# Linear attention and an MLP mixer on one core: the second batch's loads moved from SyncE's queue to GpSimd's, between the weight pieces

## The chip, the cores and the metric

The kernel runs on one core of one Trainium2 chip. The time is the device time of one execution in microseconds (us). A profiled execution gives a trace of every instruction and of every DMA packet; its times run from the first instruction. TensorE is called PE, VectorE DVE, ScalarE ACT, GpSimd POOL and SyncE SP.

## The reference

```python
# attention, for q, k, v of 8 batches x 8 heads x 576 positions x 64
phi = lambda x: np.where(x > 0, x, np.exp(x) - 1.0) + 1.0
q_p, k_p = phi(q), phi(k)
kv  = np.einsum('bhsd,bhse->bhde', k_p, v)
z   = np.sum(k_p, axis=2)
num = np.einsum('bhsd,bhde->bhse', q_p, kv)
den = np.einsum('bhsd,bhd->bhs', q_p, z)[..., None] + 1e-06
x = (num / den), heads joined to 8 x 576 x 512
# mixer: w_tok1 576x256, w_tok2 256x576, w_ch1 512x1536, w_ch2 1536x512
h = np.maximum(x.transpose(0, 2, 1) @ w_tok1, 0.0) @ w_tok2
u = x + h.transpose(0, 2, 1)
out = u + np.maximum(u @ w_ch1, 0.0) @ w_ch2
```

All inputs and the output are float32.

## The kernel before

**Staging.** The work goes batch by batch (n = 0 to 7), with the next batch's attention laid into the matmuls of this batch's channel mixer. Each batch reads q, k and v in two halves, c = 0 and 1, of 576 KB each (four heads to a half). A half of k or q goes through ACT's exponential (`phi_exp`, L248), DVE's max(x, 0) + 1 (`phi_add`, L252) and DVE's minimum of the two (`phi_end`, L258). A half of v is cast to bf16 into `vs` (`vcast`, L271), on DVE where `ON_DVE` names it (1v0) and else on ACT (1v1). PE then transposes the q halves (`qtr_mm`, L316), forms kv (L298, tokens 1K) and the numerators.

**Names in the order.** `ORDER` (L65) is a hand-kept list of some 1,100 tokens, run in sequence under a manual schedule; each engine and each issuing queue takes its own instructions in that order. `1Lk0` issues the load of batch 1, k, half 0. `1kx0`, `1ka0` and `1kb0` are its three phi steps, `1v1` is the cast of v half 1, `1Q..` are the transposes and `1K` is kv. `0ma5` and `0mb5` are the two halves of the first channel product for columns 640 to 767 (L682), `0r5` reads it back with relu. `0q0` to `0q11` are the second channel product of batch 0 (L743). `G01` and the like are DVE's sums of blocks of w_ch1 (L893), for a product scheme with seven multiplications. `Aw00`, `Aw11`, `Aw01` and `Aw10` copy w_tok2 into `w2p` in another order, the first two on POOL, the others on DVE (L661). `A38`, `A39`, `A43` and `A40` are the products that read `w2p` (L634). `A19` is a pair of warm-up matmuls on zeros (L1088), which stand in the buffer that v of batch 1 is loaded to.

**The loads.** Batch 0's k and q halves are issued by SP. POOL issues v of batch 0 (in bf16, two halves) and all weights, which it converts from float32 to bf16 on the way: w_tok1, a small half of its last row (`w1t`), w_tok2, w_ch1 in four pieces of 384 columns (`load_wc1`, L1115, all rows), the other half of `w1t` (L1134), and w_ch2 in four pieces of 384 rows (`load_wc2`, L1120). A w_ch1 or w_ch2 piece is 768 KB read and 384 KB written. Of a piece i of w_ch1, columns 384 i to 384 i + 383 come; block sums `G0.` need pieces 0 and 2. A piece of w_ch2 serves three of `0q0` to `0q11`.

Later batches' loads are issued by SP through `load` (L221). Two tables put waits in front of loads: `GATE` makes SP hold 1k0 until w_ch1 piece 0 has landed, and 2q0 until w_ch2 piece 1 has; `WGATE` makes POOL hold w_ch2 piece 1 until 1v1 has landed. Since a queue is in order, what stands behind a held load is held with it. Tokens `B0`, `B1` and `B2` issue w_ch2 pieces 1 to 3.

POOL's transfers use eight semaphores in turn, so that each of its DMA issues waits for the eighth one before it to land; POOL's other work stands behind such a wait.

Of the kernel before, what the change touches and what calls it, by code (L numbers as in the profile page):

```python
# [64 lines left out]
ORDER = """A2 A0 A1 A3 A4 A5 A6 A8 A9 A7 A10 A12 A13 A14 A11 A16 A17 A15 1Lk0 Aw11 A21 Aw00 A20 A19 1Lk1 1Lv1 A23 A18 A22 A25 A26  # L65
A29 1Lq0 A24 A28 A27 A32 A30 A31 A32l A33 A34 A35 A36 A37 Aw01 Aw10 A38 A39 A43 A40 0gt A41 A42 At3 G01 G02 At2 0ma5
0ma4 0ma1 G03 0mb1 0gv 0r1 G04 0ma7 0mb7 0r7 1kx0 0mb4 0r4 0mb5 0ma2 0mb2 0ma0 1ka0 1kb0 0mb0 0ma8 0mb8 G21 G22 G24
0r0 0r5 0ma11 G23 0ma3 G11 G12 G13 1ka1 0r8 1Lq1 1Lv0 B0 B1 B2 0mb3 0r3 0mb11 0r11 0ma6 0ma9 0mb9 0mb6 0r2 0r6 0q0
1kx1 1v1 0r9 1qx0 1kb1 0q1 2Lq0 1qa0 1qb0 1qx1 0ma10 0mb10 1Q01 1Q00 0r10 1qa1 0q2 1Qc00 1Qc01 ws02 1qb1 1Q11 1Q10 1v0
1K 1Kc0 1Qc10 2Lq1 0q3 1Qc11 1Kc1 1n20 2Lv0 1n01 0q4 0q5 1nc01 1n00 0q6 2qx0 2qx1 2v0 1nc20 2Lk0 1nc00 1n10 0q7 1n11  # L70
2Lk1 0q8 0q9 1nc10 1nc11 1n21 0q10 2qa0 1nc21 1f0 1fr0 1f1 1fr1 ws04 2kx1 2qb0 2qa1 ws14 0q11 wt2 1h01 1h00 2qb1 0z1
1hu00 1h11 2Lv1 3Lq0 1h10 0z0 1hu01 1hu11 1t0 1t1 1g2 1hu10 1t2 1tc1 1t3 1tc0 1ma3 1ma1 1tc2 1tc3 1mb1 2qT1 2qT0 2kx0
1ma8 1ma4 3qx0 1mb4 0z3 3Lq1 1r1 1r4 1gu2 0ut 1ma2 1mb2 1mb3 1ma5 1mb5 1mb8 2ka0 1r3 ws24 2v1 2kb0 1ma9 2ka1 2kb1 0uc
3qx1 2K 2Kc1 3Lk1 1r2 0z2 1ma7 1mb7 2Kc0 ws00 ws10 3qa0 1r7 1mb9 1r9 3qb0 1ma0 1mb0 1r8 ws12 2n 3Lv0 1r5 ws34 1ma11
1mb11 2nd 2o1 1r0 2n1 T01 1r11 2ne 1ma6 2n0 1mb6 1p10 3v0 2n2 1ma10 1mb10 2o0 2f0 3Lk0 1r6 1r10 1p20 1p21 0o1 1p11
3Lv1 1w10 ws22 2fr0 3qa1 wt0 4Lv0 3qb1 1w20 T02 3kx0 1w13 2f1 4Lq1 3ka0 T00 G14 ws32 ws20 1c0 Tr02 3kx1 1w30 3kb0 1w23
1p50 ws30 3qT1 1w40 3qT0 3ka1 3kb1 1p51 2fr1 2g1 Tr01 Tr00 0o0 1c2 4qx1 2g0 1p60 2gu0 2uT0 1p30 3v1 2gu1 2uT1 4qa1
1p61 1eZ 3K 1hZ 1c1 3Kc1 1p31 1eY 1p70 3Kc0 1p71 3n 1eW 4Lv1 4v0 3nd 3ne 3o0 U00 4Lk0 U01 1p41 U02 3o1 3n1 2x01 4Lk1
2x11 2y01 3n2 1p40 3n0 2x12 2s1 2s2 2x02 V0 1eX 4Lq0 2y11 2x16 2y12 5Lv0 2s3 2y02 2x15 4v1 4qb1 2x06 2y16 4kx0 2x21
2x05 2y21 1hW 4ka0 2x17 2y15 2y17 4kb0 3f0 4qa0 5Lk0 2s4 3f1 2x26 2y06 2x07 2y05 2y07 4qx0 5Lq0 4qb0 4qT0 3fr0 4ka1  # L80
2x25 3fr1 1hY 2y26 1o 2y25 2x14 2x13 2y13 3gt 2x27 2y27 2x22 2y22 2x23 2x03 2y03 2p10 2y14 4kx1 4kb1 2x04 2y04 2x24
4qT1 3g0 2y23 2w10 3g1 2y24 2w12 2p20 2w20 2w22 2p11 2w30 3gu1 2p50 2p51 2c0 2p60 3uT1 3gt1 2p61 3gu0 2p21 2c1 3gt0
3uT0 4K 2eZ 2p70 4Kc1 2c2 2w40 3ut 2p71 4Kc0 4n 2eW 5Lq1 2p30 4nd 2hW 5Lk1 4ne 2p31 5Lv1 4n0 2p41 2hZ 4o0 4n1 2p40
3x11 3s1 3x21 4o1 3y11 3s2 3x01 4n2 5kx0 3x16 3x12 2eY 3y21 T12 3s3 5v0 2eX 2hY 3x15 3y12 3x05 3y16 3x02 5ka0 2o 3y01
3x26 3y02 6Lk0 3x25 3x06 5kb0 3y25 W0 3x22 3y26 5ka1 3x23 3y06 3x17 3y22 3y15 3x27 3s4 3y05 3x07 3y17 5kx1 T11 3y27
3x03 3y07 Tr12 6Lk1 3x14 Tr11 3y03 3x24 5kb1 3x13 3y24 4f0 3y13 5qx0 5qa0 4f1 3y14 3y23 4fr0 5qb0 3x04 4fr1 T10 3w12
3y04 5qa1 4g0 Tr10 3w10 5v1 4g1 4gu0 5qx1 3p20 4gu1 4uT0 5K 6kx1 3p21 3w20 4uT1 5qb1 3p10 5Kc1 6kx0 3w22 3p11 5qT1 3eZ
3p50 3c0 6ka1 3p51 5Kc0 5qT0 3w40 U10 3c2 3w30 U11 6Lq0 6Lq1 6kb1 U12 4s1 6ka0 3p31 V1 3p30 7Lk0 4s2 6Lv1 3p61 3eY
6Lv0 3p60 6kb0 7Lk1 5n 3c1 5nd 3hY 3p71 5ne 3p70 5n0 3hZ 4x02 5o0 3eW 4x01 4x21 5n2 4y01 3hW 3p40 4y21 4y02 4x06 6qx0
5n1 4x05 4x26 4y06 6qa1 3p41 4y05 5o1 4x11 4s3 4x03 3eX 4y11 4x25 4y26 4s4 3o 4x07 4y03 6qx1 4x12 4y07 4x16 4x27 4y25  # L90
4y12 4x04 4y16 6qb1 5f0 4y04 6qa0 6v0 4x15 4y27 4x23 4w10 4y15 4x17 6qb0 5fr0 4x22 4y17 4x13 6qT0 4x24 4y23 4x14 4y24
4y13 6qT1 5f1 4y14 4y22 6v1 7ka1 4p20 4w12 4p21 5fr1 4w20 5g1 4w22 4p10 5gu1 4p11 5g0 4w40 5uT1 4c0 4eZ 5gt 6K 5gu0
4hZ 4p50 6Kc1 6Kc0 5gt1 5uT0 7kx1 4p51 5gt0 4p60 4c2 4w30 7Lv0 6n 7kx0 7Lq0 7kb1 4p61 7Lq1 6ne 7Lv1 4p30 6nd 4c1 6n2
4p31 4p71 6n0 4p70 4eY 5x11 6o1 5x02 6o0 5y11 5s1 5x12 4eW 5x01 5s2 5x15 5y01 4hW 6n1 4p40 7v0 5x16 5y12 4p41 5y16
7ka0 5x06 5y15 5s3 5x21 5y02 7F12 5x13 5y21 4eX 4hY 5x17 5y06 5x05 5y17 5x26 5y05 7kb0 4o 5x07 5y26 5x25 5y13 5x03
5y25 5s4 5x27 7qa0 7qx0 6f0 5y07 7v1 7qb0 5x14 6f1 7qa1 7qx1 5y27 5x04 6fr0 5y03 5x22 6fr1 5x23 7qb1 5y14 5x24 5y22
5y04 7qT1 7K 5y23 5p10 7Kc1 7Kc0 5w10 7qT0 5y24 6g0 5w30 6g1 5w12 5w20 5p20 6gu1 5p50 5p11 5w22 6uT1 6gu0 5p21 5c0
5p51 5eZ 6uT0 5p60 5c2 5w40 7n 5hZ 7nd 5p61 7ne 5p31 7n1 5c1 7F15 5p30 7o1 7o0 5p70 7n2 5p71 6s1 5eY 6x21 6x01 6s2 5hY
7n0 6x11 6y01 6x12 6y11 6x06 6y21 6s3 6x15 5eW 6y06 6x16 6x02 5hW 6y16 6x05 6y02 5p40 6y12 7F14 6x26 6s4 6y15 6x17
7F11 6x25 6y26 6x07 7F10 6y05 5p41 6y25 W1 6x13 5eX 6x03 6y07 6x23 7F13 6x27 6y03 6x22 5o 6x04 6y22 7f0 6y17 6y23 7f1  # L100
7fr0 6y27 6y04 6x14 6y13 7fr1 6x24 6y14 6w30 7g0 6y24 6w10 6p10 7gu0 7g1 6w12 7uT0 6p11 6w20 6p50 6w22 6c0 5ut 6p20
7gu1 6p51 7F2 7uT1 7gt 6p61 7gt0 6p60 6w40 7x12 6c1 7gt1 6p21 6c2 7F4 7ut 6p71 6eZ 7x11 6p70 7s1 6hZ 7x02 6eW 7x01
# [9 lines left out]
def kernel(  # L112
# [108 lines left out]
    def load(nm, n, c, gate=None):  # L221
        src_ = src[nm][n].rearrange("(j a) (p t) d -> (a p) j (t d)", a=2, t=T)
        js = slice(2 * c, 2 * c + 2)
        return after(nc.sync.dma_start(out=raw[nm, rb(n)][:, js], in_=src_[:, js]), gate)
# [887 lines left out]
    NB = 4  # L1112
    CB = DCH // NB

    def load_wc1(i):  # L1115
# [1 line left out]
        return nc.gpsimd.dma_start(
            out=wc1[:, :, cs], in_=moe_w_ch1[:, cs].rearrange("(k p) c -> p k c", p=128))
# [76 lines left out]
```

## Time and profile before

| What | us |
|---|---|
| median of 3 runs (lowest, highest) | 245.59 (244.32, 246.74) |
| the profiled execution: its own time | 243.56 |
| its span, first to last instruction | 241.8 |
| PE busy in the span | 233.3 (97%) |
| DVE, ACT, POOL busy | 213.3, 136.6, 77.1 |
| DMA: share of 16 engines of SP's queue, of POOL's | 51.2%, 24.7% |

The granted TensorE clock was 0.999 of full. Busy time is that of instructions; waits and DMA issues show in other views. In a line of the timeline the first number is the start, the second the length of a run of like instructions; the bracket gives the idle time in front of it and what ended that. A line of a DMA issue tells when it was issued, not when the data landed; the view of DMA issues has the median time to landing.

### The profile page before, as it was taken

The page shows a single profiled execution, that of the slowest core. Times are in us where ns is not written, and L with a number is a line of the kernel's source. Part 1 is how long each engine was busy: PE and PEld are TensorE (multiplying, and loading weights), DVE is VectorE, ACT ScalarE, POOL GpSimd, SP SyncE. Part 2 cuts the span into 40 slices and gives each one's busy share as a digit, 9 for nine tenths or more (in the row PEclk, how much of TensorE's full clock was granted, in tenths as well). Part 3 has the DMA queues.
Part 4 walks back from the last instruction along what each step waited for, and adds up shares of the span by engine and source line. Part 5 has one row for each costly group of instructions (what it writes and reads, how often), then busy time and mean ns, then how long its engine had stood idle before and what let it go on. Part 6 is the DMA issues. An engine that isn't in the chain of part 4 may idle for free.

```text
span 241.8 us, 6383 instructions
## 1 busy us (share of the span) xinstructions
PE 233.3 (97%) x2616; PEld 173.5 (72%) x2616; DVE 213.3 (88%) x389; ACT 136.6 (56%) x224; POOL 77.1 (32%) x86
## 2 busy tenths in 40 slices
PE   7899979999999999999999999999999999999992
PEld 3585435465687677789877887688778867888882
DVE  5987897989899899999999999999999599867662
ACT  4763781788687296237994397448923542346100
POOL 8750046173800620035100620207005820440640
PEclk9999999999999999999999999999999999999999
DMA  6999999997998999488948989494782186134026
GB/s 241 273 202 253 333 295 291 411 206 215 338 313 122 287 359 274 87 124 304 294 122 173 367 266 199 82 276 164 159 139 46 39 171 119 22 80 96 3 55 207
DMA packets 49805, 48.42 MB, mean 200 GB/s; under 512 B 30064, under 2 KB 35568, under 8 KB 49776
## 3 DMA queue, kind: packets, MB, share of 16 engines
q1 hardware_dynamic: 41664, 35.00, 51.2%
q0 software_dynamic: 7472, 12.22, 24.7%
q10 hardware_dynamic: 640, 0.79, 1.1%
q8 instruction: 20, 0.33, 0.5%
q14 instruction: 9, 0.07, 0.1%
HBM read 35.85 MB, written 9.44 MB: 187 GB/s over the span
## 4 chain that ended last, share of the span: by engine, by line
PE 83%; DMA 7%; DVE 4%; POOL 3%; issue 1%; ACT 0%; POOLq 0%; DVEq 0%; ACTq 0%
PE ps L966 27%; PE ps L924 23%; PE ps L444 6%; PE ps L743 5%; PE ps L455 4%; PE ps L682 4%; DMA wc<-in_moe_w_ch_dram 4%; DMA k_raw<-in_k_dram 3%; PE ps L707 2%; PE ps L729 2%; PE ps L298 2%; PE ps L1020 2%; PE ps L383 2%; DVE swc L893 1%; DVE y L252 1%; POOL qT L1107 1%
## 5 line engine op out<-in xcount | busy, mean ns | idle before, releaser
L966 PE MATMUL ps<-k_raw,v_raw 128*128 128x256 bf16 x252 | 31.7, 273 | 0.0
L939 ACT COPY v_raw<-ps 128x512 f32<-128x512 f32 x30 | 16.9, 595 | 23.0 <-PE ps L924 21.7
L966 PEld LDWEIGHTS <-cr 128*128 128x128 bf16 x252 | 24.4, 98 | 5.3 <-DVE cr L677 0.3
L966 PEld LDWEIGHTS <-v_raw 128*128 128x128 bf16 x252 | 24.1, 98 | 3.6 <-issue 0.4
L924 PEld LDWEIGHTS <-swc 128*128 128x128 bf16 x240 | 23.3, 98 | 3.5 <-issue 0.4
L1067 POOL TENSOR_TENSOR obuf<-obuf,q_raw 128x512 f32<-128x512 f32 x6 | 8.2, 1373 | 48.7 <-DVE obuf L1060 48.7
L677 DVE CUSTOM_DVE_ANT_0 cr<-ps,v_raw 128x512 bf16<-128x512 f32 x30 | 20.1, 685 | 4.1 <-ACT v_raw L939 2.1
L924 PEld LDWEIGHTS <-wc 128*128 128x128 bf16 x216 | 21.1, 98 | 3.6
L924 PE MATMUL ps<-crt,swc 128*128 128x256 bf16 x180 | 23.3, 273 | 0.0
L248 ACT ACTIVATE e<-q_raw 128x1152 bf16<-128x1152 f32 x16 | 18.7, 1167 | 6.8 <-DVE x L360 4.8
L682 PE MATMUL ps<-uT,wc 128*128 128x512 bf16 x96 | 22.1, 380 | 0.0
L966 PE MATMUL ps<-wc,cr 128*128 128x256 bf16 x168 | 21.6, 273 | 0.0
L248 ACT ACTIVATE e<-k_raw 128x1152 bf16<-128x1152 f32 x16 | 18.7, 1170 | 3.2 <-DMA k_raw<-in_k_dram 3.1
L924 PE MATMUL ps<-uT,wc 128*128 128x256 bf16 x144 | 19.5, 273 | 0.0
L1060 DVE TENSOR_TENSOR obuf<-ps,u 128x512 f32<-128x512 f32 x24 | 16.4, 685 | 2.9 <-PE ps L966 2.7
L409 DVE TENSOR_TENSOR x<-ps,dens 128x768 bf16<-128x768 f32 x18 | 16.5, 934 | 0.0
L1067 POOL TENSOR_TENSOR obuf<-obuf,part 128x512 f32<-128x512 f32 x6 | 7.7, 1287 | 27.1 <-DVE dens L396 18.6
L1067 POOL TENSOR_TENSOR obuf<-obuf,w 128x512 f32<-128x512 f32 x6 | 7.8, 1292 | 26.3 <-ACT w L1054 19.5
L682 PEld LDWEIGHTS <-wc 128*128 128x128 bf16 x96 | 9.0, 98 | 9.8
L466 DVE TENSOR_TENSOR u<-ps,x 128x1024 bf16<-128x1024 f32 x12 | 14.5, 1220 | 0.3 <-PE ps L455 0.2
L832 DVE TENSOR_TENSOR v_raw<-cr 128x512 bf16<-128x512 bf16 (+3 forms) x24 | 14.4, 619 | 0.0
L444 PE MATMUL ps<-x,w 128*128 128x512 bf16 x56 | 14.4, 379 | 0.0
(169 smaller groups left out, 510.2 us busy)
## 6 DMA issues: line engine op xcount, KB each, us to landing
k_raw<-in_k_dram SPq DMA_DIRECT2D x16, 576.0 KB, 6.5
q_raw<-in_q_dram SPq DMA_DIRECT2D x16, 576.0 KB, 6.0
v_raw<-in_v_dram SPq DMA_DIRECT2D x14, 576.0 KB, 7.2
out_dram<-obuf POOLq DMA_DIRECT2D x12, 512.0 KB, 5.8
wc<-in_moe_w_ch_dram POOLq DMA_DIRECT2D x8, 384.0 KB, 9.9
out_dram<-obuf POOLq DMA_DIRECT2D x4, 256.0 KB, 6.9
cr<-in_v_dram POOLq DMA_DIRECT2D x2, 288.0 KB, 7.5
out_dram<-obuf POOLq DMA_DIRECT2D x4, 128.0 KB, 4.8
```

What stands on the lines that cost most here:

```text
L248: nc.scalar.activation(out=ebuf[EBUF[f"{n}{nm}{c}"]], in_=f, func=AF.Exp)
L409: nc.vector.tensor_tensor(out=xv[:, :, rc0:rc0 + 3], in0=nd_tile(n, m)[:, :, k0:k0 + 6, 0:D].rearrange("p i (q a) d -> p i q a d", a=2), i ...
L444: nc.tensor.matmul(out=banks(f"{n}f")[:, mt], lhsT=w1t[:, b, ms] if r == R else w1[:, r, ms], rhs=x[b][:, r, :], start=(r == 0), stop=(r = ...
L466: nc.vector.tensor_tensor(out=u[b][:, rs], in0=banks(f"{n}g{i}"), in1=x[b][:, rs], op=ALU.add)
L677: nc.vector._custom_dve(TENSOR_ADD_SAT, out=o, in0=ps, in1=c, s0=3.4028234663852886e38, s1=0.0)
L682: nc.tensor.matmul(out=bank(f"{n}m{mc}"), lhsT=wc1[:, kj, 128 * mc:128 * mc + 128], rhs=uTj[b][:, kj] if n < 2 - U1 else uT[b][:, :, kj], ...
L832: return engine.tensor_tensor(out=s_[which - 1][:, ks], in0=x_, in1=y_, op=op)
L924: nc.tensor.matmul(out=ps[:, j], lhsT=lhs[:, k_, 128 * j:128 * (j + 1)], rhs=rhs[:, :, k_], start=(first and j == 0 and k_ == 0), stop=(k_ ...
L939: nc.scalar.copy(out={1: c1, 6: c6, 5: c5}[i], in_=ps)
L966: nc.tensor.matmul(out=ps, lhsT=lhs[:, k_], rhs=rhs[:, k_], start=(first and not skip and k_ == 0), stop=(k_ == KH - 1), skip_group_check= ...
L1060: nc.vector.tensor_tensor(out=slots(f"{n}P", 4)[:, d::2, HC[c]], in0=pair_tile(n, "X" if z == "W" else z), in1=u[n % 2][:, d::2, HC[c]], o ...
L1067: nc.gpsimd.tensor_tensor(out=o, in0=o, in1=part[i], op=ALU.add)
```

## The change

The six loads of batch 1 go out from POOL's queue, in a given place among the weight pieces, and the two gates that held 1k0 and w_ch2 piece 1 go.

```diff
-GATE = {'1k0': ('wc1', 0), '2q0': ('wc2', 1), '4q0': ('u', 2, 1), '7q0': ('u', 5, 1)}
-WGATE = {1: ('in', 'v', 1, 1)}
+GATE = {'2q0': ('wc2', 1), '4q0': ('u', 2, 1), '7q0': ('u', 5, 1)}
+WGATE = {}

-ORDER = """... A16 A17 A15 1Lk0 Aw11 A21 Aw00 A20 A19 1Lk1 1Lv1 A23 A18 A22 A25 A26
-A29 1Lq0 A24 A28 ...
-0ma4 0ma1 G03 0mb1 0gv 0r1 G04 0ma7 0mb7 0r7 1kx0 ...
-... 1ka1 0r8 1Lq1 1Lv0 B0 B1 B2 0mb3 0r3 ...
+ORDER = """... A16 A17 A15 A19 1Lk0 P2 1Lk1 P3 Pt 1Lq0 Aw00 Aw11 Pw 1Lq1 1Lv1 1Lv0
+B0 B1 B2 A21 A20 A23 A18 A22 A25 A26 A29 A24 A28 ...
+0ma4 0ma1 G03 0mb1 0gv 0r1 G04 0ma7 0mb7 0r7 1kx0 ...
+... 1ka1 0r8 0mb3 0r3 ...

     def load(nm, n, c, gate=None):
...
-        return after(nc.sync.dma_start(out=raw[nm, rb(n)][:, js], in_=src_[:, js]), gate)
+        queue = nc.gpsimd if n == 1 else nc.sync
+        return after(queue.dma_start(out=raw[nm, rb(n)][:, js], in_=src_[:, js]), gate)
...
-    for i in range(NB):
-        live["wc1", i] = load_wc1(i)
-    nc.gpsimd.dma_start(out=w1t[half[1], 1, :], in_=w1r[:, 2 * R])
-    load_wc2(0)
+    for i in range(2):
+        load_wc1(i)
+    for i in range(2, NB):
+        put(f"P{i}", load_wc1, i)
+    put("Pt", lambda: nc.gpsimd.dma_start(out=w1t[half[1], 1, :], in_=w1r[:, 2 * R]))
+    put("Pw", load_wc2, 0)
```

So POOL issues, after w_ch1 pieces 0 and 1: 1k0, w_ch1 2, 1k1, w_ch1 3, the rest of `w1t`, 1q0, the copies `Aw00` and `Aw11`, w_ch2 0, 1q1, 1v1, 1v0, w_ch2 1, 2 and 3. The warm-up pair `A19` moves ahead of `A20`, the first batch's kv of its first half (`kv_first(0)`, L565). The rest of the order is kept: DVE and ACT run the same instructions in the same sequence, ACT's being 1kx1, 1v1, 1qx0, 1qx1. SP's queue holds, after batch 0's four loads, the loads of batch 2 onwards.

More of the change, by code (lines that the diff above doesn't have):

```diff
@@ L63 @@
 4k1:0 5k0:0 5k1:0 5q0:0 5q1:0 6k1:0 6k0:0 6q1:0 6q0:0 7k1:0 7k0:0 7q0:0 7q1:0 25465:241833""".split())}
[L65 to L98, printed above, removed]
@@ L99 @@
-7n0 6x11 6y01 6x12 6y11 6x06 6y21 6s3 6x15 5eW 6y06 6x16 6x02 5hW 6y16 6x05 6y02 5p40 6y12 7F14 6x26 6s4 6y15 6x17
+ORDER = """A2 A0 A1 A3 A4 A5 A6 A8 A9 A7 A10 A12 A13 A14 A11 A16 A17 A15 A19 1Lk0 P2 1Lk1 P3 Pt 1Lq0 Aw00 Aw11 Pw 1Lq1 1Lv1 1Lv0
+B0 B1 B2 A21 A20 A23 A18 A22 A25 A26 A29 A24 A28 A27 A32 A30 A31 A32l A33 A34 A35 A36 A37 Aw01 Aw10 A38 A39 A43 A40
+0gt A41 A42 At3 G01 G02 At2 0ma5 0ma4 0ma1 G03 0mb1 0gv 0r1 G04 0ma7 0mb7 0r7 1kx0 0mb4 0r4 0mb5 0ma2 0mb2 0ma0 1ka0
+1kb0 0mb0 0ma8 0mb8 G21 G22 G24 0r0 0r5 0ma11 G23 0ma3 G11 G12 G13 1ka1 0r8 0mb3 0r3 0mb11 0r11 0ma6 0ma9 0mb9 0mb6
@@ new lines @@
+0r2 0r6 0q0 1kx1 1v1 0r9 1qx0 1kb1 0q1 2Lq0 1qa0 1qb0 1qx1 0ma10 0mb10 1Q01 1Q00 0r10 1qa1 0q2 1Qc00 1Qc01 ws02 1qb1
+1Q11 1Q10 1v0 1K 1Kc0 1Qc10 2Lq1 0q3 1Qc11 1Kc1 1n20 2Lv0 1n01 0q4 0q5 1nc01 1n00 0q6 2qx0 2qx1 2v0 1nc20 2Lk0 1nc00
+1n10 0q7 1n11 2Lk1 0q8 0q9 1nc10 1nc11 1n21 0q10 2qa0 1nc21 1f0 1fr0 1f1 1fr1 ws04 2kx1 2qb0 2qa1 ws14 0q11 wt2 1h01
+1h00 2qb1 0z1 1hu00 1h11 2Lv1 3Lq0 1h10 0z0 1hu01 1hu11 1t0 1t1 1g2 1hu10 1t2 1tc1 1t3 1tc0 1ma3 1ma1 1tc2 1tc3 1mb1
+2qT1 2qT0 2kx0 1ma8 1ma4 3qx0 1mb4 0z3 3Lq1 1r1 1r4 1gu2 0ut 1ma2 1mb2 1mb3 1ma5 1mb5 1mb8 2ka0 1r3 ws24 2v1 2kb0 1ma9
@@ new lines @@
+2ka1 2kb1 0uc 3qx1 2K 2Kc1 3Lk1 1r2 0z2 1ma7 1mb7 2Kc0 ws00 ws10 3qa0 1r7 1mb9 1r9 3qb0 1ma0 1mb0 1r8 ws12 2n 3Lv0 1r5
+ws34 1ma11 1mb11 2nd 2o1 1r0 2n1 T01 1r11 2ne 1ma6 2n0 1mb6 1p10 3v0 2n2 1ma10 1mb10 2o0 2f0 3Lk0 1r6 1r10 1p20 1p21
+0o1 1p11 3Lv1 1w10 ws22 2fr0 3qa1 wt0 4Lv0 3qb1 1w20 T02 3kx0 1w13 2f1 4Lq1 3ka0 T00 G14 ws32 ws20 1c0 Tr02 3kx1 1w30
+3kb0 1w23 1p50 ws30 3qT1 1w40 3qT0 3ka1 3kb1 1p51 2fr1 2g1 Tr01 Tr00 0o0 1c2 4qx1 2g0 1p60 2gu0 2uT0 1p30 3v1 2gu1
+2uT1 4qa1 1p61 1eZ 3K 1hZ 1c1 3Kc1 1p31 1eY 1p70 3Kc0 1p71 3n 1eW 4Lv1 4v0 3nd 3ne 3o0 U00 4Lk0 U01 1p41 U02 3o1 3n1
@@ new lines @@
+2x01 4Lk1 2x11 2y01 3n2 1p40 3n0 2x12 2s1 2s2 2x02 V0 1eX 4Lq0 2y11 2x16 2y12 5Lv0 2s3 2y02 2x15 4v1 4qb1 2x06 2y16
+4kx0 2x21 2x05 2y21 1hW 4ka0 2x17 2y15 2y17 4kb0 3f0 4qa0 5Lk0 2s4 3f1 2x26 2y06 2x07 2y05 2y07 4qx0 5Lq0 4qb0 4qT0
+3fr0 4ka1 2x25 3fr1 1hY 2y26 1o 2y25 2x14 2x13 2y13 3gt 2x27 2y27 2x22 2y22 2x23 2x03 2y03 2p10 2y14 4kx1 4kb1 2x04
+2y04 2x24 4qT1 3g0 2y23 2w10 3g1 2y24 2w12 2p20 2w20 2w22 2p11 2w30 3gu1 2p50 2p51 2c0 2p60 3uT1 3gt1 2p61 3gu0 2p21
+2c1 3gt0 3uT0 4K 2eZ 2p70 4Kc1 2c2 2w40 3ut 2p71 4Kc0 4n 2eW 5Lq1 2p30 4nd 2hW 5Lk1 4ne 2p31 5Lv1 4n0 2p41 2hZ 4o0 4n1
@@ new lines @@
+2p40 3x11 3s1 3x21 4o1 3y11 3s2 3x01 4n2 5kx0 3x16 3x12 2eY 3y21 T12 3s3 5v0 2eX 2hY 3x15 3y12 3x05 3y16 3x02 5ka0 2o
+3y01 3x26 3y02 6Lk0 3x25 3x06 5kb0 3y25 W0 3x22 3y26 5ka1 3x23 3y06 3x17 3y22 3y15 3x27 3s4 3y05 3x07 3y17 5kx1 T11
+3y27 3x03 3y07 Tr12 6Lk1 3x14 Tr11 3y03 3x24 5kb1 3x13 3y24 4f0 3y13 5qx0 5qa0 4f1 3y14 3y23 4fr0 5qb0 3x04 4fr1 T10
+3w12 3y04 5qa1 4g0 Tr10 3w10 5v1 4g1 4gu0 5qx1 3p20 4gu1 4uT0 5K 6kx1 3p21 3w20 4uT1 5qb1 3p10 5Kc1 6kx0 3w22 3p11
+5qT1 3eZ 3p50 3c0 6ka1 3p51 5Kc0 5qT0 3w40 U10 3c2 3w30 U11 6Lq0 6Lq1 6kb1 U12 4s1 6ka0 3p31 V1 3p30 7Lk0 4s2 6Lv1
@@ new lines @@
+3p61 3eY 6Lv0 3p60 6kb0 7Lk1 5n 3c1 5nd 3hY 3p71 5ne 3p70 5n0 3hZ 4x02 5o0 3eW 4x01 4x21 5n2 4y01 3hW 3p40 4y21 4y02
+4x06 6qx0 5n1 4x05 4x26 4y06 6qa1 3p41 4y05 5o1 4x11 4s3 4x03 3eX 4y11 4x25 4y26 4s4 3o 4x07 4y03 6qx1 4x12 4y07 4x16
+4x27 4y25 4y12 4x04 4y16 6qb1 5f0 4y04 6qa0 6v0 4x15 4y27 4x23 4w10 4y15 4x17 6qb0 5fr0 4x22 4y17 4x13 6qT0 4x24 4y23
+4x14 4y24 4y13 6qT1 5f1 4y14 4y22 6v1 7ka1 4p20 4w12 4p21 5fr1 4w20 5g1 4w22 4p10 5gu1 4p11 5g0 4w40 5uT1 4c0 4eZ 5gt
+6K 5gu0 4hZ 4p50 6Kc1 6Kc0 5gt1 5uT0 7kx1 4p51 5gt0 4p60 4c2 4w30 7Lv0 6n 7kx0 7Lq0 7kb1 4p61 7Lq1 6ne 7Lv1 4p30 6nd
@@ new lines @@
+4c1 6n2 4p31 4p71 6n0 4p70 4eY 5x11 6o1 5x02 6o0 5y11 5s1 5x12 4eW 5x01 5s2 5x15 5y01 4hW 6n1 4p40 7v0 5x16 5y12 4p41
+5y16 7ka0 5x06 5y15 5s3 5x21 5y02 7F12 5x13 5y21 4eX 4hY 5x17 5y06 5x05 5y17 5x26 5y05 7kb0 4o 5x07 5y26 5x25 5y13
+5x03 5y25 5s4 5x27 7qa0 7qx0 6f0 5y07 7v1 7qb0 5x14 6f1 7qa1 7qx1 5y27 5x04 6fr0 5y03 5x22 6fr1 5x23 7qb1 5y14 5x24
+5y22 5y04 7qT1 7K 5y23 5p10 7Kc1 7Kc0 5w10 7qT0 5y24 6g0 5w30 6g1 5w12 5w20 5p20 6gu1 5p50 5p11 5w22 6uT1 6gu0 5p21
+5c0 5p51 5eZ 6uT0 5p60 5c2 5w40 7n 5hZ 7nd 5p61 7ne 5p31 7n1 5c1 7F15 5p30 7o1 7o0 5p70 7n2 5p71 6s1 5eY 6x21 6x01 6s2
@@ L100 @@
+5hY 7n0 6x11 6y01 6x12 6y11 6x06 6y21 6s3 6x15 5eW 6y06 6x16 6x02 5hW 6y16 6x05 6y02 5p40 6y12 7F14 6x26 6s4 6y15 6x17
 7F11 6x25 6y26 6x07 7F10 6y05 5p41 6y25 W1 6x13 5eX 6x03 6y07 6x23 7F13 6x27 6y03 6x22 5o 6x04 6y22 7f0 6y17 6y23 7f1
```

## The prediction

> **What bounds the kernel now.** I read the busy time by stage first, to see where TensorE (PE) idles at all; columns are the stretch, its length, then busy us of PE, its weight loads, VectorE (DVE), ScalarE (ACT) and GpSimd (POOL), granted clock, DMA share, GB/s.
>
> ```profile
> 26.00:30.00 4.00, 4.00 (x20) 1.82 (x19) 3.90 (x10) 3.19 (x7) 0.00 (x0) 1.00 1.09 349
> 30.00:32.00 2.00, 1.29 (x7) 0.48 (x5) 2.00 (x4) 1.84 (x3) 1.03 (x2) 1.00 1.04 400
> 32.00:34.00 2.00, 1.69 (x8) 0.59 (x6) 1.86 (x3) 1.70 (x2) 1.46 (x2) 1.00 0.96 304
> 34.00:36.00 2.00, 1.74 (x17) 1.02 (x18) 1.86 (x4) 2.00 (x4) 0.00 (x0) 1.00 1.22 203
> 36.00:60.00 24.00, 24.00 (x294) 13.67 (x292) 21.15 (x43) 15.57 (x24) 10.76 (x11) 1.00 1.00 278
> 60.00:230.00 170.00, 170.00 (x1971) 135.20 (x1970) 157.39 (x276) 96.75 (x158) 47.59 (x49) 1.00 0.70 180
> ```
>
> From 36 to 230 us PE is never idle, so no later slack can win back a delay made before 36 us, and only the 0.71 + 0.31 + 0.26 = 1.28 us of idle in 30 to 36 us can be won there. The DMA engines are full (share about 1) to that point: it is a question of which bytes come first. Next, the timeline of PE (start, length, what; in brackets the wait before it and what ended it):
>
> ```profile
> 20.57 9.66 PE L682 MATMUL ps<-uT,wc 128*128 128x512 bf16 x44
> 30.94 1.89 PE L743 MATMUL ps<-wc,cr 128*128 128x512 bf16 x8 [0.71 <-DMA wc<-in_moe_w_ch_dram]
> 32.66 1.03 PE L682 MATMUL ps<-uT,wc 128*128 128x512 bf16 x4
> 34.14 0.68 PE L316 MATMUL ps<-identity,qp 128*128 128x128 bf16 x9 [0.45 <-DVE qp L258]
> ...
> 36.47 0.71 PE L298 MATMUL ps<-vs,kp 64*64 64x65 bf16 x64
> ```
>
> and of ACT, which feeds the transposes at 34.14, with the loads' issues on SP and POOL that feed ACT and PE:
>
> ```profile
> 29.52 1.17 ACT L248 ACTIVATE e<-k_raw 128x1152 bf16<-128x1152 f32 x1
> 30.57 1.15 ACT L271 CAST vs<-v_raw 128x1152 bf16<-128x1152 f32 x1
> 31.88 1.17 ACT L248 ACTIVATE e<-q_raw 128x1152 bf16<-128x1152 f32 x1 [0.16 <-DMA q_raw<-in_q_dram]
> 33.35 1.16 ACT L248 ACTIVATE e<-q_raw 128x1152 bf16<-128x1152 f32 x1 [0.30 <-DMA q_raw<-in_q_dram]
> ```
>
> ```profile
> 17.80 0.88 SPq L224 DMA_DIRECT2D k_raw<-in_k_dram  x2
> 18.73 0.47 SPq L224 DMA_DIRECT2D v_raw<-in_v_dram  x1
> 19.24 0.98 SPq L224 DMA_DIRECT2D q_raw<-in_q_dram  x2
> ```
>
> ```profile
> 11.07 0.74 POOL L1117 DMA_DIRECT2D wc<-in_moe_w_ch_dram  x1 [0.99 <-DMA cr<-in_v_dram]
> ...
> 15.26 1.54 POOL L661 COPY w2p<-w 128x320 bf16<-128x320 bf16 x2 [0.43 <-DMA w<-in_moe_w_tok_dram]
> ```
>
> See that ACT takes the value half 1v1 (30.57) before both query halves (31.88, 33.35), and that SP now issues 1v1 before 1q0 and 1q1.
>
> **Landings before and after.** Adding each issue's time to landing (DMA view by window): wc1 pieces 0 to 3 land at 17.8, 19.5, 21.5 and 26.0; 1k0 24.5, 1k1 28.4, 1v1 30.4, wc2 piece 0 30.9, 1q0 31.8, 1q1 33.3, 1v0 34.7, wc2 piece 1 36.8 (SP's gated issue of 2q0). Prices follow. A wc1 piece with its queue alone takes 1.9 us (17.8, 19.5, 21.5). A 576 KB load on SP's queue takes 1.45 us (batch two: issued 36.8 to 38.8, landing 42.8, 44.3, 45.6, 47.0, 48.4). A wc2 piece takes 2.05 (36.8, 38.9, 40.9).
>
> After the change SP's queue is empty from the first four loads until wc2 piece 1 lands, and one queue carries all: wc1 1 at 19.6, 1k0 21.1, wc1 2 23.0, 1k1 24.4, wc1 3 26.3, the small w1t half 26.5, 1q0 28.0, wc2 0 30.0, 1q1 31.5, **1v1 33.0**, 1v0 34.4, wc2 1 36.5. The total is the same bytes in the same time; the order differs.
>
> **Part by part.**
>
> *Gates removed.* SP's wait for wc1 0 and POOL's 14.2 us wait for 1v1 go. The chain's 6.74 us for 1k0 (17.80 to 24.54) goes: 1k0 is 3.4 us earlier. Late next is wc1 2.
>
> *Six issues move from SP to POOL.* POOL issues cost 0.54 to 0.86 us each, SP's 0.37 to 0.5. Each POOL issue also waits for the eighth POOL transfer before it (eight semaphores): 1k0 for v0 (about 11.1), 1q0 for w2 (15.2), 1v1 for 1k0 (21.1). Queued behind them on POOL are two w2p copies, once at 15.26, now after 1q0's issue: 15.6 + 0.75, so from 16.35, ends 17.1 and 17.9 (Aw00 now first). The second block of L634 products then starts 0.6 us late. Cover: PE waits for wc1 2 next. About seven transfers, 10 us, are ahead of each issue, so POOL's issue time itself costs nothing; were it stalled, that backlog must run out first.
>
> *One warm-up matmul pair moves ahead of kv_first(0).* At most 0.46 us (two steps of 0.23 from L1088, four in 1.11 us) on the first batch's chain; same cover. A gain is excluded, since it only goes ahead of work.
>
> *1k0 ahead of wc1 2.* 21.5 becomes 23.0. PE's fifth group of L682, 0ma7, is due at 20.57 + 4 x 0.44 = 22.3, so it starts 1.0 late (23.3); this covers the two delays above. DVE's first swc sum (21.48, which waited for the same piece) starts at 23.1, but 1k0's exponential was at 24.62 and moves 0.3 only. The 44 matmuls end near 31.2, wc2 0 is there at 30.0, and the 0.71 us wait is gone: PE's L743 starts at 31.2 against 30.94, +0.3. L682's last group ends near 33.9.
>
> *1q0 and 1q1 ahead of 1v1.* ACT, 1.0 late through PE, ends 1k1's exponential near 31.6 and then sits until 33.0, with 1q0 long landed behind it. The cast starts at 33.1 (+2.5). The first query exponential came 1.31 later, 0.16 of it waiting for data: now 33.1 + 1.15 = 34.25, **+2.35**. DVE's end of it and PE's transposes follow: 34.14 becomes 36.5, PE idle 2.6 us. The second half keeps the same spacing (compute-bound by DVE: 33.33 to 34.98 for its two ends), 1v0 is there at 34.4, so L298 at 36.47 becomes 38.8. wc2 1 is due after that and landed at 36.5. After it PE has work without pause, so 2.35 us stays.
>
> **Sum.** 1.0 for wc1 2, less 0.71 for wc2 0, is inside the 2.35, not added. The profiled execution's own time is 243.56 (span 241.8 and 1.8 around it): 243.56 + 2.35 = 245.9. It lay 2.03 below the median of 245.59; on the median, 247.9. I forecast that, 0.96% slower.
>
> The unknown is a plain f32 load's rate on POOL's queue, which before never makes one. Nearest rows: v0's two halves on that queue, 576 KB read each, land 1.65 us apart (10.85, 12.5) while sharing the engines; on SP's queue loads land 1.45 apart, at best 1.33 (4.54, 5.87). Five loads go up to 1v1's landing, itself included: 1.33 gives 0.6 less, +1.75; 1.65 gives 1.0 more, +3.35. Far row: out_dram stores of 512 KB on POOL's queue land 5.8 us after issue, two of them together, so at most 2.9 each: 7.25 more, +9.6. I take 1.45, the row of the same shape and bytes with its queue alone.
>
> **Rivals.**
> 1. *1v1 in time*: it lands by 31.6, so ACT never sits, and only wc1 2 costs, +1.0 through ACT: 244.6, on the median 246.6. For: 1.33 a load brings it to 32.4. Against: even that is 0.8 too late.
> 2. *Loads on POOL's queue are slower*, or POOL's issues stall past the backlog: v0's 1.65 a load gives +3.35: 246.9, median 248.95; far end 253.2 and 255.2. For: two POOL issues of 1.15 and 1.01 against 0.74. Against: the others hold 0.74 with DVE 88% busy (4.41 of 5 us in 10 to 15). [...]
> 3. *The clock falls in the new 2.6 us idle.* Price from rows: the PE work from the transposes to the end of L298, 34.14 to 37.2, at half speed costs up to 3.1 more: +4 to +5.45, I take +4.7: 248.3, median 250.3. Decides from: an idle long enough; the longest here after the start, 0.71, kept 1.00. [...]
> 4. *Not slower*: the queue without mixing runs faster. If 1v1 lands by 30.5, 2.5 earlier, and the pieces with it, the waits from 30.94 on go, at most 1.28 us: 242.3, median 244.3. It needs 12.7 us where I have 15.2 from wc1 0 on, a 20% better rate; share and GB/s (400 at 30 to 32 us) speak against.
>
> **Numbers.** About 1% is what a measurement of this kernel can tell from no change: bounds 243.1 and 248.05 on the median. Forecast 0.58, split about its mid 247.9 by some 0.6 for the landing and 1 for the runs: 0.32 within, 0.26 slower. Rival 1 0.11, within. Rival 2 0.14 and 3 0.07, slower. Rival 4 0.10: 0.06 within, 0.04 faster. So faster 0.04, within 0.49, slower 0.47. The range 245.6 to 250.4 reaches rival 1 less 1.0 for the runs and rival 3; it leaves out rival 4 and rival 2's far end.
>
> **What would show it.** Right: L682's 44 matmuls broken by a wait for wc near 22.5; no 0.71 wait at L743; ACT's cast of v_raw waiting some 1.4 us for in_v_dram until 33; PE idle over 2 us before L316; L298 at 38.8; nothing idle after. Wrong: v_raw landing before 31.6, loads spaced over 1.7 us, a clock under 1.00, or a gap after 40 us.

## The result, and the profile after

The changed kernel takes 247.04 us (median of 17 runs, 246.43 to 249.06); the kernel before, timed beside it, 245.28 us (17 runs, 244.03 to 247.53). The ratio is 1.0077, 95% interval 1.0049 to 1.0105: slower by 1.2 to 2.6 us. The forecast was 247.9, slower by 2.35.

The profiled execution after took 247.04 us with a span of 245.2. That of before took 243.56, less than any of its 17 runs here; so of the 3.48 us between the two profiles some 1.7 (245.28 - 243.56) belongs to that one quick execution of before, not to the change; where the other runs of before lose it, no trace shows. Of the 3.4 us between the two spans, 2.8 lie ahead of kv (L299) and 0.6 behind the last weight load, where before's profiled execution ends sooner than after's. Times on the traces are compared for their places, and the medians for the size.

Line numbers after are one higher than before from L224 on, as far as they are named here: L743 is now L744, L298 is L299.

The timeline of PE after (start, length, what, count; in brackets the wait before it and what ended it):

```profile
23.30 7.94 PE L683 MATMUL ps<-uT,wc 128*128 128x512 bf16 x36 [0.58 <-DMA wc<-in_moe_w_ch_dram]
31.08 1.89 PE L744 MATMUL ps<-wc,cr 128*128 128x512 bf16 x8
...
35.99 0.68 PE L317 MATMUL ps<-identity,qp 128*128 128x128 bf16 x9 [2.16 <-DVE qp L259]
...
39.27 0.78 PE L299 MATMUL ps<-vs,kp 64*64 64x65 bf16 x72 [0.95 <-DVE vs L272]
```

The 0.71 us wait of L743 for w_ch2 piece 0 is gone: L744 has no bracket. A wait of 2.16 us before the transposes (L317) and one of 0.95 before kv (L299) stand in its place. L299 starts at 39.27; before, its line stood at 36.47. Every weight load from L299 to the end comes 2.8 us later than the same one before.

Where the first wait comes from, in the timeline of ACT after:

```profile
32.92 1.16 ACT L272 CAST vs<-v_raw 128x1152 bf16<-128x1152 f32 x1 [1.23 <-DMA v_raw<-in_v_dram]
33.98 2.21 ACT L249 ACTIVATE e<-q_raw 128x1152 bf16<-128x1152 f32 x2
```

ACT stands 1.23 us for 1v1, and the two query exponentials run back to back behind the cast, with no wait for data of their own. Where the second wait comes from, in the timelines of DVE and of POOL after:

```profile
35.96 0.76 DVE L253 TENSOR_SCALAR y<-q_raw 128x1152 bf16<-128x1152 f32 x1
...
37.50 1.72 DVE L272 CAST vs<-v_raw 128x1152 bf16<-128x1152 f32 x1
```

```profile
36.86 3.36 POOL L813 TENSOR_TENSOR q_raw<-wc 128x512 f32<-128x512 bf16 x2 [8.45 <-DVE y L253]
```

The cast of 1v0 takes 1.72 us, where the same instruction took 0.76 before, and the two POOL sums of weights at L813 take 3.36 where they took 2.26. The same two in the timelines of DVE and of POOL before:

```profile
35.66 0.76 DVE L271 CAST vs<-v_raw 128x1152 bf16<-128x1152 f32 x1
```

```profile
36.90 2.26 POOL L812 TENSOR_TENSOR q_raw<-wc 128x512 f32<-128x512 bf16 x2 [3.44 <-DMA wc<-in_moe_w_ch_dram]
```

Before, POOL's sums started when that cast had ended. Now the sums are released by the y step of 1q1 (`phi_add`; bracket: DVE y L253), which has become late with the query exponentials, and so they start in the middle of DVE's last steps towards kv.

In the last view, busy time by stage (stretch, its length, then PE, its weight loads, DVE, ACT, POOL, clock, DMA share, GB/s), the lost time lies in two stretches, and after 40 us PE is busy again nearly throughout:

```profile
34.00:36.00 2.00, 0.01 (x1) 0.02 (x2) 0.82 (x3) 2.00 (x3) 0.00 (x0) 1.00 1.24 205
...
38.00:40.00 2.00, 1.05 (x79) 0.83 (x77) 1.94 (x3) 0.00 (x0) 2.00 (x2) 1.00 1.10 339
40.00:60.00 20.00, 19.84 (x137) 11.24 (x133) 17.23 (x36) 12.85 (x19) 7.11 (x7) 1.00 0.70 236
```

**The theory** for the runs: the loss is ACT's cast standing in order ahead of two query exponentials whose data is there. The rivals: w_ch1 piece 2 behind 1k0 costs the time; loads on POOL's queue are slow in themselves; the cast of 1v0 beside POOL's sums costs the time; the clock falls in PE's new idle.

### The profile page after: what moved, and what is told of

Its sections match the earlier page's. It is cut to its first block, busy times and chain, and to the rows that moved or that the text cites. A ratio compares the mean times of both kernels' runs of the same rounds, so it can differ in the third digit from the quotient of the medians.

```text
span 245.2 us, 6359 instructions
## 1 busy us (share of the span) xinstructions
PE 233.0 (95%) x2598; PEld 173.9 (71%) x2616; DVE 214.7 (88%) x389; ACT 136.7 (56%) x224; POOL 82.9 (34%) x92
## 4 chain that ended last, share of the span: by engine, by line
PE 82%; DMA 12%; DVE 2%; issue 1%; POOL 1%; ACT 0%; POOLq 0%; DVEq 0%
PE ps L967 27%; PE ps L925 23%; PE ps L445 6%; PE ps L744 5%; DMA v_raw<-in_v_dram 5%; PE ps L456 4%; DMA k_raw<-in_k_dram 4%; PE ps L683 4%; DMA cr<-in_v_dram 3%; PE ps L708 2%; PE ps L730 2%; PE ps L299 2%; PE ps L1021 2%; PE ps L384 2%; POOL qT L1108 1%
## 5 line engine op out<-in xcount | busy, mean ns | idle before, releaser
L925 PEld LDWEIGHTS <-swc 128*128 128x128 bf16 x240 | 23.3, 98 | 3.5 <-issue 0.4
L925 PEld LDWEIGHTS <-wc 128*128 128x128 bf16 x216 | 21.1, 98 | 3.6
L925 PE MATMUL ps<-crt,swc 128*128 128x256 bf16 x180 | 23.3, 273 | 0.0
L683 PE MATMUL ps<-uT,wc 128*128 128x512 bf16 x91 | 21.6, 379 | 1.0 <-DMA wc<-in_moe_w_ch_dram 0.6
L683 PEld LDWEIGHTS <-wc 128*128 128x128 bf16 x96 | 9.0, 98 | 10.6 <-DMA wc<-in_moe_w_ch_dram 1.1
L272 ACT CAST vs<-v_raw 128x1152 bf16<-128x1152 f32 x12 | 13.9, 1156 | 1.6 <-DMA v_raw<-in_v_dram 1.6
```

Of the source, the lines that this page charges most:

```text
L683: nc.tensor.matmul(out=bank(f"{n}m{mc}"), lhsT=wc1[:, kj, 128 * mc:128 * mc + 128], rhs=uTj[b][:, kj] if n < 2 - U1 else uT[b][:, :, kj], ...
L925: nc.tensor.matmul(out=ps[:, j], lhsT=lhs[:, k_, 128 * j:128 * (j + 1)], rhs=rhs[:, :, k_], start=(first and j == 0 and k_ == 0), stop=(k_ ...
```

## The experiments

All ratios are to the kernel before, run beside it on the same chip (244.5 to 244.8 us). Each edit is made to the kernel after, unless it is said otherwise.

### e1: 1v1 loaded ahead of the queries

```diff
-... P3 Pt 1Lq0 Aw00 Aw11 Pw 1Lq1 1Lv1 1Lv0
+... P3 Pt 1Lv1 Aw00 Aw11 Pw 1Lq0 1Lq1 1Lv0
```

> The changed kernel, with only the load of value half 1v1 issued ahead of 1q0 and 1q1 on POOL's queue (1k0, wc1 2, 1k1, wc1 3, w1t, 1v1, wc2 0, 1q0, 1q1, 1v0). Theory (ACT sits behind 1v1, which lands after both query halves): 1v1 lands near 28, ACT's cast no longer waits, 1q0 lands at 31.5 in time, PE's transposes start about 1.4 us earlier than in the changed kernel and L299 moves from 39.3 to about 37.9, or 37.2 if the cast of 1v0 is also no longer slowed; what stays against the kernel before is the 1.0 us from wc1 piece 2. Time 1.2 to 2.0 us below the changed kernel, about the kernel before plus 0 to 1. Rival (the whole loss comes from wc1 piece 2 standing behind 1k0): no change against the changed kernel, 247.

Measured: 244.78 us, ratio 1.0000 (0.9976 to 1.0024). The timelines of ACT, PE and DVE in e1:

```profile
31.30 1.15 ACT L272 CAST vs<-v_raw 128x1152 bf16<-128x1152 f32 x1
```

```profile
34.67 0.68 PE L317 MATMUL ps<-identity,qp 128*128 128x128 bf16 x9 [1.12 <-DVE qp L259]
...
37.00 0.78 PE L299 MATMUL ps<-vs,kp 64*64 64x65 bf16 x72
```

```profile
36.19 0.76 DVE L272 CAST vs<-v_raw 128x1152 bf16<-128x1152 f32 x1
```

The cast of 1v1 waits for nothing, and the loss is gone, with all six loads still on POOL's queue and 1k0 still ahead of w_ch1 piece 2. So POOL's queue costs nothing by itself that the ratio can tell, which is 0.6 us to either side; in the profile L299 is still 0.53 us later than before (37.00, not 36.47). The cast of 1v0 is back at 0.76 too.

### e2 and e12: w_ch1 piece 2 ahead of 1k0, alone and with e1

```diff
-... A15 A19 1Lk0 P2 1Lk1 P3 ...
+... A15 A19 P2 1Lk0 1Lk1 P3 ...
```

e2 is this alone:

> The changed kernel, with only wc1 piece 2 issued ahead of 1k0. Theory (ACT sits behind 1v1): wc1 2 lands at 21.5 again, the waits of PE's L683 and DVE's first swc sum near 23 go, but 1v1 still lands near 33, so the cast stays at about 33 and the time stays that of the changed kernel within 0.4 us. Rival (wc1 piece 2 carries the loss): 1.0 us or more faster than the changed kernel.

Measured: 247.25 us, ratio 1.0094 (1.0062 to 1.0126), as after. The timeline of PE in e2:

```profile
30.50 1.89 PE L744 MATMUL ps<-wc,cr 128*128 128x512 bf16 x8
...
35.84 0.91 PE L317 MATMUL ps<-identity,qp 128*128 128x128 bf16 x9 [2.58 <-DVE qp L259]
36.53 1.91 PE L744 MATMUL ps<-wc,cr 128*128 128x512 bf16 x4
```

PE comes to L744 0.58 us earlier than after (30.50, not 31.08), and loses that again waiting for the same late query half: idle 2.58 instead of 2.16, and L299 is at 39.34, as after. What comes next is slow: four matmuls of L744 take 1.91 where they take 1.03 elsewhere. The stages in e2 say why, in the column of the clock:

```profile
36.00:38.00 2.00, 2.00 (x13) 1.14 (x12) 1.90 (x3) 1.70 (x4) 1.28 (x1) 0.53 1.24 205
38.00:40.00 2.00, 2.00 (x83) 1.56 (x80) 1.62 (x3) 0.00 (x0) 2.00 (x2) 0.61 1.12 344
```

The granted clock is 0.53 and 0.61 in the two stretches behind the idle: at half speed (0.50 in stages of h1) that is an estimated 2 x (0.47 + 0.39) / 0.5 = 3.4 us. All six runs of e2 have a mean clock of 0.990 to 0.992, against 0.995 or more in the runs of before beside it. That is the third rival of the prediction, in a kernel that differs little from the changed one.

e12 has e2's and e1's edits:

> Both edits: wc1 piece 2 ahead of 1k0, and 1v1 ahead of 1q0 and 1q1. Theory: neither wait is left, wc2 0 still lands at 30 instead of 30.9, 1q0 at 31.5 and 1q1 at 33.0, so L299 starts near 36.2 and the time is that of the kernel before or up to 0.6 us below it. Rival (POOL's queue itself is slower for float32 loads, or the DVE and POOL work collide anyway): the time stays 1 us or more above the kernel before.

Measured: 244.42 us, ratio 0.9993 (0.997 to 1.0015). The timeline of PE in e12:

```profile
30.36 1.89 PE L744 MATMUL ps<-wc,cr 128*128 128x512 bf16 x8
...
34.23 0.68 PE L317 MATMUL ps<-identity,qp 128*128 128x128 bf16 x9 [1.11 <-DVE qp L259]
...
36.56 0.78 PE L299 MATMUL ps<-vs,kp 64*64 64x65 bf16 x72
```

With both, L744 starts 0.58 us earlier than before (30.36, not 30.94) and nothing of that reaches L299 (36.56, not 36.47): 1.11 us of idle before L317 take the place of before's 0.71 + 0.45. The piece ahead of 1k0 is worth 0.44 us at L299 (37.00 to 36.56), which the ratios can't tell from nothing.

### e3, f1 and f2: the collision and the clock, one at a time and together

e3 keeps POOL's sums off the cast of 1v0: they come after it in the order, and depend on it.

```diff
-... 0q2 1Qc00 1Qc01 ws02 1qb1
-1Q11 1Q10 1v0 1K ...
+... 0q2 1Qc00 1Qc01 1qb1
+1Q11 1Q10 1v0 ws02 1K ...
-        copy(out=vs[:, js, :, 0:D],
+        live["cast", n, c] = copy(out=vs[:, js, :, 0:D],
-        first = {... (2, 0): ("phi", "k", 2, 1)}.get((i, k0))
+        first = {... (2, 0): ("phi", "k", 2, 1), (0, 2): ("cast", 1, 0)}.get((i, k0))
```

> The changed kernel, with POOL's first pair of w_ch2 block sums (L813 at 36.9) made to wait for DVE's cast of 1v0. In the changed kernel that cast took 1.72 us where other casts of this shape on DVE took 0.76, and POOL's pair took 3.36 where it took 2.26 before, both at once. Theory (the two hold each other up): the cast takes 0.76 again, L299 starts 0.9 us earlier, and the time is 0.9 us below the changed kernel. Rival (the cast was slow by itself, or by the DMA): it stays at 1.7 and the time does not move.

Measured: 247.06 us, ratio 1.0078 (1.0049 to 1.0108): no gain. The timeline of PE in e3:

```profile
35.55 0.74 PE L317 MATMUL ps<-identity,qp 128*128 128x128 bf16 x9 [2.37 <-DVE qp L259]
36.08 1.91 PE L744 MATMUL ps<-wc,cr 128*128 128x512 bf16 x4
...
38.88 0.99 PE L299 MATMUL ps<-vs,kp 64*64 64x65 bf16 x72
```

The collision is gone (the cast takes 0.76 again, and POOL's sums, now from 37.96 on, 2.27), but the clock has fallen (a mean of 0.51 in 36 to 38 us and 0.64 in 38 to 40; 1.91 us for four matmuls), and it sets L299 instead. The twelve runs of e3 differ in just this: eight have a mean clock of 0.990 to 0.992 (3.4 us at half speed out of 245 lower the mean by 0.007) and a median of 247.2 us; four have 0.996 or 0.997 and a median of 245.8. By this the fall of the clock costs 1.4 us where nothing else is in the way. For runs without a trace the mean clock does not tell where the fall lay; that it is this one is inferred.

f1 keeps the collision and takes away the idle: eight matmuls of 512 columns between L683's last group and L317. Their result is never used.

```diff
-... 0ma10 0mb10 1Q01 ...
+... 0ma10 0mb10 fill 1Q01 ...
+    def fill():
+        for i in range(8):
+            nc.tensor.matmul(out=psum[:, 2], lhsT=identity, rhs=wc1[:, i % 4, 0:512], start=True, stop=True)
```

> The changed kernel, with eight matmuls of 512 columns (1.7 us, results not used) put into PE's idle time ahead of the transposes L317. They change no data and wait for nothing late. Theory (after the idle there are two losses side by side: in some executions the granted clock falls to half at 36 us for 3.4 us, and DVE's cast of 1v0 collides with POOL's sums; the later of the two sets L299): the clock stays at 1.00, but the cast still takes 1.7 us, so L299 stays near 39.2 and the time stays within 0.4 us of the changed kernel. Rival (the clock is what costs): 0.8 us or more below the changed kernel.

Measured: 246.85 us, ratio 1.0088 (1.0056 to 1.012). All eleven runs have a clock of 0.994 or more, and the time is that of after. The timeline of PE in f1 names what sets it now:

```profile
38.63 0.78 PE L299 MATMUL ps<-vs,kp 64*64 64x65 bf16 x72 [0.95 <-DVE vs L272]
```

f2 has both edits:

> The same eight matmuls, and POOL's sums made to wait for the cast of 1v0 as well. Theory (two losses side by side): with both gone L299 starts near 38.1 and the time is 0.8 to 1.2 us below the changed kernel, where either edit alone gave about nothing; what is left against the kernel before is the wait for 1v1, about 1.4 us of the 2.35 that were forecast or less. Rival (they are not what cost time): as the changed kernel.

Measured: 245.96 us, ratio 1.0049 (1.0019 to 1.0078), full clock. The timeline of PE in f2:

```profile
38.19 0.78 PE L299 MATMUL ps<-vs,kp 64*64 64x65 bf16 x72
```

Here nothing waits at L299. Neither cure alone gains anything; both together gain 0.9 us on f1, run beside it (runs from 245.7 to 246.9 against 246.4 to 247.8; the intervals of the two ratios overlap, since both hold the spread of before). These are two waits side by side in front of L299: the later of them counts. This is also why the runs of after show no mark of the clock: nine of its seventeen have a mean clock of 0.990 to 0.992 and a median of 247.03, six have 0.995 to 0.999 and a median of 247.00. (Two with 0.982 took 248.6 and 249.1.) The four runs of e3 that kept the clock agree: 245.8, as f2's 245.96. What is left in f2, 1.2 us, is the late query exponential itself: L299 stands at 38.19, and at 37.00 in e1, where the exponential is not late.

### g1: the loads as after, the cast later on ACT

```diff
-0r2 0r6 0q0 1kx1 1v1 0r9 1qx0 1kb1 0q1 2Lq0 1qa0 1qb0 1qx1 0ma10 ...
+0r2 0r6 0q0 1kx1 0r9 1qx0 1kb1 0q1 2Lq0 1qa0 1qb0 1qx1 1v1 0ma10 ...
```

> The changed kernel with its loads as they are, and ACT's order changed instead: the cast of 1v1 behind the two query exponentials. Theory (the order of landing and ACT's order contradict each other; either may be turned): the exponentials start near 31.7 without waiting, the cast near 34, L299 at 37.0 to 37.5, and the time is 1.5 to 2.2 us below the changed kernel, like the version with 1v1 loaded first. Rival (the bytes simply come too late, whatever the order): within 0.5 us of the changed kernel.

Measured: 244.91 us, ratio 1.0001 (0.9971 to 1.003). The timelines of ACT and PE in g1:

```profile
31.35 1.16 ACT L249 ACTIVATE e<-q_raw 128x1152 bf16<-128x1152 f32 x1
```

```profile
37.05 0.78 PE L299 MATMUL ps<-vs,kp 64*64 64x65 bf16 x72
```

The first query exponential waits for nothing, the cast comes at 34.11, after both, and kv 2.2 us earlier than after. Not one transfer is moved here, and the loss is gone. So the change's loads aren't late for the kernel's need; they come in an order that ACT's instructions don't have. Putting either into the other's order gives before's time, within 0.3%.

### h1: what the gates were for

The kernel before, with SP's loads, and both gates taken out:

```diff
-GATE = {'1k0': ('wc1', 0), '2q0': ('wc2', 1), ...}
-WGATE = {1: ('in', 'v', 1, 1)}
+GATE = {'2q0': ('wc2', 1), ...}
+WGATE = {}
```

> The kernel before with its loads on SP, and only the two gates taken away (1k0 no longer waits for wc1 piece 0, wc2 piece 1 no longer for 1v1). Theory (the DMA engines are full from 2 to 41 us, so a queue's place in time decides whose bytes come first): batch 1's 3.5 MB go out from 3 us on and share the engines with v0, w_tok1, w_tok2 and wc1 0 and 1; PE's L682 starts 4 to 6 us late and the time is 248.5 to 251.5. Rival (gates cost and do nothing, since all bytes are needed by 41 us anyway): the time of the kernel before or below.

Measured: 254.3 us, ratio 1.0372 (1.0311 to 1.0432), more than any theory allowed. The timeline of PE in h1, with before's line numbers:

```profile
20.56 1.01 PE L623 MATMUL ps<-x,w 128*128 128x256 bf16 x4 [2.64 <-DMA w<-in_moe_w_tok_dram]
...
29.41 9.92 PE L682 MATMUL ps<-uT,wc 128*128 128x512 bf16 x43
```

and one of its stages:

```profile
20.00:24.00 4.00, 3.44 (x17) 2.48 (x18) 0.00 (x0) 0.60 (x1) 0.75 (x1) 0.50 1.13 296
```

All but one of the second batch's loads go out by 5.9 us and share the DMA engines with v of batch 0 and w_tok1 (a median of 9.6 and 13.1 us from issue to landing, where before has 7.5 and 7.4), for which PE waits 1.38 + 0.93 + 2.64 us; the clock is 0.50 from 16 to 24 us, and 0.92 and 0.80 in the 4 us to either side, by which it stands at half from 15.4 to 25.6 us. L682 starts 8.8 us late; 4 to 6 had been expected, and the expectation had nothing for the clock. So the gates of before aren't free to leave out with the loads on SP. The changed kernel has no such gates either, and e1 has before's time: there the place in POOL's queue does their work.

### i1: the engines' order turned to that of the landings

e2's queue; ACT takes 1qx0, 1kx1, 1qx1, 1v1, 1v0, and DVE the two query halves ahead of 1k1's.

```diff
-ON_DVE = {'1v0', '2v1', ...}
+ON_DVE = {'2v1', ...}
-EBUF ... 1q1:2
+EBUF ... 1q1:1
-... G13 1ka1 0r8 ... 0q0 1kx1 1v1 0r9 1qx0 1kb1 0q1 2Lq0 1qa0 1qb0 1qx1 0ma10 0mb10 1Q01 1Q00 0r10 1qa1
-0q2 1Qc00 1Qc01 ws02 1qb1 1Q11 1Q10 1v0 1K ...
+... G13 1qa0 0r8 ... 0q0 1qx0 1kx1 0r9 1qb0 0q1 2Lq0 1qx1 1qa1 1v1 1qb1 0ma10 0mb10 1ka1 1Q01 1Q00 1kb1 1v0
+0r10 0q2 1Qc00 1Qc01 ws02 1Q11 1Q10 1K ...
```

> The kernel after with w_ch1 piece 2 ahead of 1k0 (as in the run e2), and with the order of ACT and DVE turned to that of the landings: ACT takes 1qx0, 1kx1, 1qx1, 1v1, 1v0 (1v0 moves from DVE to ACT), DVE takes the two query halves' phi steps ahead of 1k1's; the exponential of 1q1 gets 1k0's buffer, which is free by then. Theory (the loss is one query exponential queued behind late data, and behind it DVE and ACT, both busy from 28 to 36 us, are what is left): in e12 DVE's chain of half 1k1, two query halves and the cast of 1v0 starts at 31.8 and ends at 36.5, and L299 starts at 36.56. With the query halves first and the cast gone from DVE, the first end of a query half starts near 31.9, L317 can follow L683's last group at 33.0 with no idle, the second L317 is near 34.6, kp is ready near 35.7 and L299 starts at 35.5 to 36.0: 0.6 to 1.0 us earlier than in e12, so 243.4 to 243.9 where before is 244.5, ratio 0.995 to 0.998. Rival (the order of the DMA is the limit whatever the engines do): 1v1 and 1v0 land at 32.8 and 34.2 and ACT casts both one after the other, ending at 35.4; if ACT's other work pushes them later, L299 is at 36.5 or later and the time is that of before, ratio 0.999 to 1.002. Second rival (the collision moves): POOL's sums L813 start when w_ch2 piece 1 lands (36.2), when DVE has only copies of PSUM left, so no stretch of L259 beyond 0.80.

Measured: 245.02 us, ratio 1.0012 (0.9978 to 1.0046): the gain did not come. The timeline of PE in i1:

```profile
33.30 0.67 PE L317 MATMUL ps<-identity,qp 128*128 128x128 bf16 x9
...
36.06 0.66 PE L317 MATMUL ps<-identity,qp 128*128 128x128 bf16 x9 [1.24 <-ACT cr L692]
...
37.13 0.78 PE L299 MATMUL ps<-vs,kp 64*64 64x65 bf16 x71 [0.26 <-ACT qT L323]
```

The first transposes have no wait any more, as expected (33.30), but the second ones wait for ACT's 0r10 and kv for ACT's copies out of PSUM, which I hadn't counted and which now stand behind two casts. The chain of waits runs through ACT from 32.3 to 37.1 us without a gap: exponential, two casts, 0r10, two copies. The theory's rest, that ACT and DVE are what is left, holds; that their order alone could give 0.6 to 1.0 us is refuted for this order. Orders with these copies ahead of the casts weren't tried.

## Why the prediction was right, point by point

**Gates, issues and the warm-up pair at no cost: right.** 1k0 was issued at 10.96, with POOL issues of 0.71 to 0.77 us for the loads and pieces up to 1v0, as priced, and 1v1 at 21.61, behind the landing of 1k0, as forecast (21.1). e1 and g1 have all of this and before's time, within the intervals.

**1k0 ahead of w_ch1 piece 2: right.** 0ma7 starts at 23.30 (forecast 23.3), L744 at 31.08 (31.2), without the 0.71 us wait. e2 shows that this step is covered: without it the time is not lower, though there the clock's fall may hide something; e1 with the step and e12 without it are 0.44 us apart at L299, and their ratios can't be told apart.

**1v1 at 33.0, ACT behind it: right.** The cast starts at 32.92 (forecast 33.1), the first query exponential at 33.98 (34.25), L317 at 35.99 (36.5). L317 came 0.5 us sooner than worked out, in part because the exponential did. e1 and g1 undo this step alone, by the transfers or by ACT's order, and each brings the time back to before's: this cause is shown. With the wait, they also take away what follows from it, the collision and the long idle.

**"L298 at 36.47 becomes 38.8": right within 0.5, by a sum that lacked one term.** L317 came 0.5 earlier than worked out and the cast of 1v0 took 0.96 longer; L299 started at 39.27. I had followed what releases DVE's steps, and not what else they release: the same y step sets POOL's sums free, and a late y step puts them on the cast. By f2 the order alone costs 1.2 us (0.5 to 1.9), and the collision or the clock, whichever is later, 0.7 to 1.0 more (ratios of after and of f1 less that of f2). So the forecast's one term, 2.35, was about twice what that term measured alone, and a term that the sum did not have made up for part of it. The mechanism was right; that the number came so near owes something to luck.

**The base.** 2.35 lies in the measured 1.2 to 2.6. The forecast (247.94 before rounding) was 0.9 us above the median of after: the medians differ by 1.76, 0.59 less, and before's median is 0.31 lower with more runs.

**Rival 1** (1v1 in time) is refuted by the 1.23 us wait. **Rival 2** (POOL's queue is slow) is refuted by e1 and e12; the forecast's 1.45 us a load holds, since 1v1 landed at 32.9 after 33.0 was worked out. In after, w_ch2 piece 1's issue, the next after 1v0's, took 1.34 us where the moved loads' took 0.71 to 0.73, and DVE's y step of 1k0 (L253) ran in it, from 25.34 to 26.08. The prediction's own two slow issues of before, 1.15 at 8.18 and 1.01 at 32.45, lie on such y steps too (from 8.27 and 32.46), so that its argument from the others, which hold 0.74 with DVE 88% busy, was too strong. Whether the y step made the issue slow is not shown. In after no engine waited for that piece. **Rival 3** (the clock) was given 0.07 as a case for itself, and its priced 4 to 5.45 us never came, though the half speed of that price is in h1's stages (0.50); but the fall is in most runs of e3 and by its mean clock in at least half of those of after, at 1.4 us where it is alone, and at nothing beside the collision. The prediction called 0.71 the longest idle of before after the start; there is one of 0.95 at 8.29, which kept the clock too. **Rival 4** is refuted: 1v1 landed at 32.9, not by 30.5, and even with the order cured (e12) the kernel is only level with before.

**Where the gain of the change went.** The queue without mixing does bring PE to w_ch2 0.4 to 0.6 us sooner in e2 and e12. From there ACT and DVE, both busy nearly without pause from 30 to 36 us (5.67 and 5.72 of the 6 us in e12), set the transposes and kv, so that nothing of it arrives. None of the nine kernels was faster than before by more than its interval.

## What to carry to other kernels

When loads are moved to another queue, compare their new order of landing with the order in which each engine's instructions use them: here ACT waited 1.23 us at the first late one, and two query exponentials behind it waited too, with their data landed. Work out in the same way what a delayed step releases on other engines, since a delay can put two instructions on top of each other that ran one after the other before, as it did with the cast of 1v0 (1.72 us, not 0.76). Where two waits stand in front of the same instruction, taking away one can show nothing, as in e3 and f1; take away both, which gave 0.9 us in f2, before calling either harmless.
